# Attention scores by two products on diagonal quarters of the array instead of one with block-diagonal queries

## The chip, the cores and the metric

One core of a Trainium2 chip runs the kernel. The metric is device time in microseconds of one execution. The runs shown of the kernel before have a median of 904.97 us (904.07 to 905.69, three runs).

## What is computed

The reference is a sparse attention, followed by a layer norm with a two-matrix feed-forward part, and a routed mixture of eight experts. Inputs are fp32: q, k and v of shape (4, 8, 576, 64), that is 4 images, 8 heads, 576 positions, 64 per head. The part that the change touches is the attention:

```python
scores = scale * np.matmul(q, k.transpose(0, 1, 3, 2))
mask_local = (rel >= 0) & (rel < stride)                     # heads 0 to 3, stride 32
mask_strided = (rel >= 0) & (pos[None, :] % stride == pos[:, None] % stride)   # heads 4 to 7
scores = np.where(masks[None, :, :, :], scores, -1000000000.0)
scores = scores - np.max(scores, axis=-1, keepdims=True)
attn = np.exp(scores)
attn = attn / (np.sum(attn, axis=-1, keepdims=True) + 1e-09)
return np.matmul(attn, v).astype(np.float32)
```

## The kernel before

The attention works on pairs of heads: image `b` and pair `hp`, where pairs 0 and 1 are local heads and pairs 2 and 3 strided ones. `GROUPS` (line 36) cuts a pair into units. A local pair has 3 units of three products, each product of 64 queries by 96 keys. A strided pair, whose positions are sorted by their remainder, has units of four, four and three products, each of 54 queries by 54 keys. An image has thus 12 units, and the four images 48.

For each pair `prep` (line 270) transposes q and k on TensorE, in two halves of 288 positions, through the PSUM tile `ps_tr`. k goes to `kT`, with both heads' 64 dimensions one above the other on 128 partitions. q goes to `qbd`, scaled: a tile with two columns per position, where head 0 fills the upper 64 partitions of the even columns and head 1 the lower 64 partitions of the odd columns. The rest of `qbd` is zero, set once at the start (lines 182 to 187). Each half of q is evacuated by two instructions, one per head (lines 290 to 294): ScalarE and then VectorE or ScalarE.

`st_scores` (line 311) makes one product of the full array for both heads (line 324): the weights are 128 columns of `qbd` for local pairs and 108 for strided ones, and `kT` moves. For images 0 and 1 a mask product goes ahead of them and the scores add to it (line 320, `MODES` in line 39); for images 2 and 3 VectorE adds the mask (line 342). The rows of a score tile alternate between the heads. `st_exp`, `st_norm` (lines 346 and 356) make the softmax. `st_trans` (line 369) transposes the weights of the softmax, 128 or 108 rows at a time, and ScalarE copies them to `pt`. `st_out` (line 385) multiplies with v: two products per group, one per head, each on 64 columns of the array, the second on PSUM partitions 64 to 127 (line 392). It reads every second column of `pt`.

Image 0 is attended first, in an order written out by hand (lines 966 to 994, kept in program order; all its instructions carry line 84). Between its steps `keep_clock` (line 300) issues filler products on an idle tile. The feed-forward part then runs over 9 chunks of 256 tokens with 16 steps each; a step has 12 products of `mm1` (line 636) and 12 of `mm2` (line 652). The units of images 1, 2 and 3 are placed between its steps by `plan` and `SPANS` (lines 51 and 1004 to 1008), and from there a scheduler orders the instructions of each engine. During the first chunks ScalarE, VectorE and GpSimd also turn the feed-forward weights from their stored form into fp32 pairs (lines 451 to 481). The routed experts follow from about 620 us.

Of the kernel before, what the change touches and what calls it, by code (L numbers as in the profile page):

```python
# [9 lines left out]
F32 = mybir.dt.float32  # L10
# [5 lines left out]
AF = mybir.ActivationFunctionType  # L16
ALU = mybir.AluOpType
# [5 lines left out]
B, H, S, DH = 4, 8, 576, 64  # L23
# [3 lines left out]
STR = 32  # L27
NA = S // STR
# [3 lines left out]
NTT = CT // TT  # L32
WL = 128 + NE + 1
QT = 96
SP = S + 18
GROUPS = (((0, 3), (3, 3), (6, 3)),) * 2 + (((0, 4), (4, 4), (8, 3)),) * 2
QW, KW = (64, 64, 54, 54), (96, 96, 54, 54)
SMW, PTW = 288, 432
# [4 lines left out]
SCALE = 1.0 / DH ** 0.5  # L43
NEG = -1.0e9
# [26 lines left out]
def attention_moe_moe(ctx: ExitStack, tc: tile.TileContext, q, k, v, g_ln, w_ch1, w_ch2, w_gate, w_local, w1, w2, out):  # L71
# [14 lines left out]
    pe, act, dve = Pin(nc.tensor), Pin(nc.scalar), Pin(nc.vector)  # L86
    pool, sp = nc.gpsimd, nc.sync
# [17 lines left out]
    pool.memset(mean_w, 1.0 / DM)  # L105
    mask_loc = cst.tile([128, 128], F32, name="mask_loc")
    pool.memset(mask_loc, 0.0)
    pool.affine_select(out=mask_loc, in_=mask_loc, pattern=[[-2, 128]], compare_op=ALU.is_ge, fill=-NEG, base=2 * STR, channel_multiplier=1)
    pool.affine_select(out=mask_loc, in_=mask_loc, pattern=[[2, 128]], compare_op=ALU.is_ge, fill=-NEG, base=-1, channel_multiplier=-1)
    mask_str = cst.tile([128, 3, NA], F32, name="mask_str")  # L110
    pool.memset(mask_str, 0.0)
    pool.affine_select(out=mask_str, in_=mask_str, pattern=[[-2 * NA, 3], [-2, NA]], compare_op=ALU.is_ge, fill=-NEG, base=0, channel_multiplier=1)
    pool.affine_select(out=mask_str, in_=mask_str, pattern=[[2 * NA, 3], [0, NA]], compare_op=ALU.is_ge, fill=-NEG, base=2 * NA - 1, channel_multiplier=-1)
    mask_str = mask_str.rearrange("p a b -> p (a b)")

    def high(ap):
# [57 lines left out]
        return ps_s["r"].tile(shape, F32, tag="s", name=name)  # L174


    qbds, kTs = [at_p.tile([128, SP, 2], F32, name="qbd")], [at_p.tile([128, SP], F32, name="kT")]
    spare = new_blk([128, 2048], F32, "spare")
    idle = spare[:, 1792:2048].bitcast(BF16)
    qbds.append(spare[:, 0:2 * SP].rearrange("p (s j) -> p s j", j=2))  # L180
    kTs.append(spare[:, 2 * SP:3 * SP])
    for qbd, kT in zip(qbds, kTs):
        pool.memset(qbd[0:64, :, 1], 0.0)
        pool.memset(qbd[64:128, :, 0], 0.0)
        pool.memset(qbd[0:64, S:SP, 0], 0.0)
        pool.memset(qbd[64:128, S:SP, 1], 0.0)
        pool.memset(kT[:, S:SP], 0.0)
    nat, vt, qTs = {}, {}, {}
    xts = {}

# [79 lines left out]
    def prep(b, hp, nm):  # L270

        odd = b == 0 and pairs.index((b, hp)) % 2
        qbd, kT = qbds[odd], kTs[odd]
        qTs[b, hp] = qbd, kT
        for half in range(2):
            t = nat.pop((nm, b, hp, half))
            ps = (ps_m.tile([128, 512], F32, tag="m", name="ps_tr")[:, 0:3 * QT] if b == 0 else side_r([128, 3 * QT], "ps_tr"))
            for i in range(3):
                pe.transpose(ps[:, QT * i:QT * i + QT], t[0:QT, i, :, :].rearrange("p h d -> p (h d)"), ident[0:QT, 0:QT])

            def dst(ap):
                if hp < 2:
                    return ap[:, 3 * QT * half:3 * QT * half + 3 * QT]
                return ap.rearrange("p (r a) -> p r a", a=NA)[:, :, NA // 2 * half:NA // 2 * half + NA // 2]

            s_ = ps if hp < 2 else ps.rearrange("p (a r) -> p r a", r=STR)
            if nm == "k":
                (act.copy if b == 0 else dve.tensor_copy)(dst(kT[:, 0:S]), s_)
            else:
                act.activation(dst(qbd[0:64, 0:S, 0]), s_[0:64], AF.Copy, scale=-SCALE)  # L290
                if half and b:
                    act.activation(dst(qbd[64:128, 0:S, 1]), s_[64:128], AF.Copy, scale=-SCALE)
                else:
                    dve.tensor_scalar(dst(qbd[64:128, 0:S, 1]), s_[64:128], -SCALE, None, op0=ALU.mult)

    sms, pts = {}, {}
    first, units = [], [0, 0]
# [5 lines left out]


    def shape_of(hp, u0):
        return dict(GROUPS[hp])[u0], QW[hp], KW[hp], 2 * QW[hp]

    def mode_of(b, hp):
        return MODES.get((b, hp), MODES.get(b, 0))
# [1 line left out]
    def st_scores(b, hp, u0):  # L311
        ng, w, n, m = shape_of(hp, u0)
        ps = side([128, ng, n], "ps_sc")
        qbd, kT = qTs[b, hp]
        mode = mode_of(b, hp)
        mask = lambda i: mask_str[0:m, 0:n] if hp > 1 else mask_loc[:, STR:STR + n] if u0 + i == 0 else mask_loc[:, 0:n]
        if mode:
            cuts = [(0, 1), (1, ng)] if hp < 2 and u0 == 0 else [(0, ng)]
            for lo, hi_ in cuts:
                pe.matmul(ps[0:m, lo:hi_, :], high(ident[0:m, 0:m]), high(mask(lo)).unsqueeze(1).to_broadcast([m, hi_ - lo, n]), start=(lo == 0), stop=False)  # L320
        for i in range(ng):
            q0 = w * (u0 + i)
            k0 = max(0, q0 - STR) if hp < 2 else q0
            pe.matmul(ps[0:m, i, :], qbd[:, q0:q0 + w, :].rearrange("p s j -> p (s j)"), kT[:, k0:k0 + n], start=not mode, stop=not mode or i == ng - 1)  # L324
        if b == 0:
            k = units[0] % SM0 * SMW
            sm = first[0][:, k:k + ng * n]
            units[0] += 1
        else:
            sm = at_p.tile([128, SMW], F32, tag="sm", bufs=SMB, name="sm")[:, 0:ng * n]  # L330
        sm = sm.rearrange("p (g n) -> p g n", g=ng)
        st = at_p.tile([128, 2, 4], F32, tag="st", bufs=5, name="st")
        sms[b, hp, u0] = (sm, st, ps)
        mn = st[0:m, 0, 0:ng]
        if mode:
            new = [lambda: dve.tensor_reduce(mn, ps[0:m], axis=AX.X, op=ALU.min)]
            if mode == 1:
                new.append(lambda: dve.tensor_tensor(sm[0:m], ps[0:m], mn.unsqueeze(2).to_broadcast([m, ng, n]), op=ALU.subtract))
            return new

        def part(i):
            dve.tensor_tensor_reduce(sm[0:m, i, :], ps[0:m, i, :], mask(i), 1.0, 3.0e38, ALU.add, ALU.min, st[0:m, 0, i:i + 1])  # L342

        return [lambda i=i: part(i) for i in range(ng)]
# [24 lines left out]
    def st_trans(b, hp, u0):  # L369
        sm, st, ps = sms.pop((b, hp, u0))  # L370
        ng, w, n, m = shape_of(hp, u0)
        ps = side([128, ng, m], "ps_pt")
        for i in range(ng):
            pe.transpose(ps[0:n, i, :], sm[0:m, i, :], ident[0:m, 0:m])
        if b == 0:
            k = SM0 * SMW + units[1] % PT0 * PTW
            pt = first[0][:, k:k + ng * m]
            units[1] += 1
        else:
            pt = at_p.tile([128, PTW], F32, tag="pt", bufs=2, name="pt")[:, 0:ng * m]  # L380
        pt = pt.rearrange("p (g m) -> p g m", g=ng)
        act.copy(pt[0:n], ps[0:n])
        pts[b, hp, u0] = pt

    def st_out(b, hp, u0):
        ng, w, n, m = shape_of(hp, u0)
        pt, vv = pts.pop((b, hp, u0)), vt.pop((b, hp, u0))
        ps = side([128, ng, w], "ps_o")
        for i in range(ng):
            k = min(w, S - w * (u0 + i)) if hp > 1 else w  # L390
            for j in range(2):
                pe.matmul(ps[64 * j:64 * j + 64, i, 0:k], vv[0:min(n, k) if hp > 1 else n, i, j, :], pt[0:min(n, k) if hp > 1 else n, i, j:2 * k:2], start=True, stop=True)
        o = ps.rearrange("p g q -> p (g q)")
        i = 0
        q0 = w * u0
        nq = min(w * ng, S - q0)
        for c in range(S * b // CT, (S * b + S - 1) // CT + 1):
            base = S * b - CT * c
            if hp < 2:
                lo, hi_ = max(q0, -base), min(q0 + nq, CT - base)  # L400
                if lo >= hi_:
                    continue
                dst = xt_of(c)[:, hp, base + lo:base + hi_]
                cut = lambda t: t[:, lo - q0:hi_ - q0]
            else:
                lo, hi_ = max(0, -base // STR), min(NA, (CT - base) // STR)
                r0, nr = q0 // NA, nq // NA
                dst = xt_of(c)[:, hp, base + STR * lo:base + STR * hi_].rearrange("p (a r) -> p r a", r=STR)[:, r0:r0 + nr, :]
                cut = lambda t: t[:, 0:nq].rearrange("p (r a) -> p r a", a=NA)[:, :, lo:hi_]
            (dve.tensor_copy if (i % 2 if b else mode_of(b, hp) > 1) else act.copy)(dst, cut(o))  # L410
            i += 1
        if b > 0:
            load_v(vq.index((b, hp, [g[0] for g in GROUPS[hp]].index(u0))) + 3)
# [1074 lines left out]
```

## Time and profile before

| | |
|---|---|
| median of the runs shown | 904.97 us |
| profiled execution | 902.98 us |
| its span, from the first instruction to the last | 901.2 us |
| mean granted TensorE clock | 0.983 |
| TensorE busy, products | 867.3 us (96%) |
| TensorE busy, weight loads | 777.3 us (86%) |
| VectorE busy | 474.5 us (53%) |
| ScalarE busy | 365.6 us (41%) |
| GpSimd busy | 152.2 us (17%) |

PE is TensorE's products, PEld its weight loads, DVE is VectorE, ACT is ScalarE, POOL is GpSimd, SP issues DMAs. A product record's duration includes the pipe behind it, so neighbours overlap; what a record costs is the distance to the next start. An fp32 product has two records, a transpose one. The granted clock is 1.00 at 2.4 GHz and 0.50 at 1.2 GHz.

### The profile page before, as it was taken

To read this page: it belongs to the slowest core of one execution; us is meant where nothing else is said; L and a number is where in the kernel's file an instruction comes from. 1 tells how busy PE (TensorE), PEld (TensorE's weight loads), DVE (VectorE), ACT (ScalarE), POOL (GpSimd) and SP (SyncE) were. 2 spreads that over 40 slices of the span, in tenths; PEclk is the share of its full clock that TensorE was granted. 3 is DMA by queue.
4 is the path that set the end of the run, shared out by engine and by line. 5 is a ranking of instruction groups with operands and counts; after the bars stand their busy time and mean duration, and the time that the engine had idled before them with its cause. 6 is when DMAs were issued, how large, how long until landed. Compare 5 with 4: busy or idle time off the path is not lost. (4 is left out here: it accounts for less than half of the span.)

```text
span 901.2 us, 17965 instructions
## 1 busy us (share of the span) xinstructions
PE 867.3 (96%) x6668; PEld 777.3 (86%) x6668; DVE 474.5 (53%) x1520; ACT 365.6 (41%) x879; POOL 152.2 (17%) x163
## 2 busy tenths in 40 slices
PE   8989888999999999999999999999999999999995
PEld 5769788999999999999999999999878787787763
DVE  4877775448766546666545555667521233111541
ACT  3688878433455234354211212332122334223550
POOL 2124323211120120120201212020231211110100
PEclk9999999899999999999999999999999999999997
DMA  9836244101212102211000000510663466410730
GB/s 190 250 106 207 59 141 121 50 14 52 65 39 46 48 10 64 47 26 39 1 1 25 1 25 6 207 49 24 239 225 101 150 218 215 139 37 24 291 113 15
DMA packets 95023, 82.91 MB, mean 92 GB/s; under 512 B 67395, under 2 KB 75589, under 8 KB 94920
## 3 DMA queue, kind: packets, MB, share of 16 engines
q1 hardware_dynamic: 87656, 65.41, 24.5%
q0 software_dynamic: 3632, 11.11, 3.7%
q10 hardware_dynamic: 3632, 5.09, 1.6%
q8 instruction: 55, 0.90, 0.4%
q14 instruction: 48, 0.39, 0.1%
HBM read 72.08 MB, written 10.30 MB: 91 GB/s over the span
## 5 line engine op out<-in xcount | busy, mean ns | idle before, releaser
L652 PE MATMUL acc<-h,w 128*128 128x256 f32 x1728 | 247.5, 291 | 1.6 <-DVE h L639 1.5
L636 PE MATMUL ps_h<-xc,w 128*128 128x256 f32 x1728 | 239.6, 287 | 0.0
L652 PEld LDWEIGHTS acc<-h,w 128*128 128x128 f32 x1728 | 220.7, 192 | 5.1 <-DVE h L639 2.5
L636 PEld LDWEIGHTS ps_h<-xc,w 128*128 128x128 f32 x1728 | 221.6, 194 | 1.7
L638 ACT ACTIVATE h<-ps_h 128x256 fp32r<-128x256 f32 x144 | 55.6, 387 | 218.3 <-PE ps_h L636 203.7
L639 DVE SCALAR_TENSOR_TENSOR h<-ps_h,h 128x256 fp32r<-128x256 f32 x144 | 60.6, 421 | 94.2 <-ACT h L638 93.5
L1367 PE MATMUL ps_h<-wx,xs 128*128 128x512 f32 x360 | 87.6, 398 | 0.8 <-DVEq L1294 0.8
L1395 PE MATMUL ps_y<-wx,ht 128*128 128x512 f32 x360 | 87.5, 399 | 0.0
L1367 PEld LDWEIGHTS ps_h<-wx,xs 128*128 128x128 f32 x360 | 66.6, 188 | 15.8 <-DVEq L1294 1.2
L1395 PEld LDWEIGHTS ps_y<-wx,ht 128*128 128x128 f32 x360 | 67.6, 191 | 13.8
L481 POOL TENSOR_TENSOR w<-stg,w 128x512 fp32r<-128x512 f32 x32 | 45.6, 1424 | 120.7 <-ACT w L480 74.5
L1398 ACT ACTIVATE y<-ps_y,pr 128x512 f32<-128x512 f32 x19 | 13.1, 687 | 90.5 <-PE ps_y L1395 54.9
L890 DVE TENSOR_TENSOR xs<-ps_tx,xs 128x512 fp32r<-128x512 f32 x15 | 10.4, 691 | 63.0 <-ACTq L1294 44.8
L1370 ACT ACTIVATE h<-ps_h 128x512 f32<-128x512 f32 x30 | 16.3, 595 | 60.8 <-PE ps_h L1367 60.8
L782 DVE TENSOR_TENSOR wx<-raw,wx 128x1024 fp32r<-128x1024 f32 x32 | 37.5, 1220 | 1.7 <-ACT wx L779 1.3
L460 ACT ACTIVATE stg<-stg 128x512 f16<-128x512 f32 x27 | 37.2, 1377 | 0.6 <-DVE stg L454 0.6
L1399 POOL DMA_INDIRECT out_dram<-y,idx x15 | 15.1, 1007 | 114.6 <-ACT y L1398 66.1
L779 ACT CAST wx<-raw 128x1024 fp32r<-128x1024 f32 x32 | 31.8, 1061 | 5.7 <-PE acc L652 4.1
L354 ACT ACTIVATE sm<-sm,st 108x54 f32<-108x54 f32 (+1 forms) x80 | 27.6, 347 | 13.5 <-DVE st L342 13.4
L1384 DVE TENSOR_TENSOR ht<-ps_th,ht 128x512 fp32r<-128x512 f32 x30 | 19.3, 685 | 24.5 <-ACT ht L1383 24.1
L324 PE MATMUL ps_sc<-kT,qbd 128*108 128x54 f32 (+1 forms) x240 | 30.5, 267 | 0.0
L892 DVE SCALAR_TENSOR_TENSOR pr<-io_e,e_rep,xg 128x8 f32<-128x8 f32 x15 | 3.4, 226 | 51.2 <-ACT y L1398 46.0
(393 smaller groups left out, 1233.7 us busy)
## 6 DMA issues: line engine op xcount, KB each, us to landing
stg<-in_moe_w_ch_dram SPq DMA_DIRECT2D x32, 512.0 KB
raw<-in_moe_w_dram SPq DMA_DIRECT2D x16, 1024.0 KB
raws<-in_moe_w_dram SPq DMA_DIRECT2D x16, 1024.0 KB
xrows<-row ACTq DMA_DIRECT2D x9, 520.0 KB
qnat<-in_q_dram SPq DMA_DIRECT2D x48, 72.0 KB
knat<-in_k_dram SPq DMA_DIRECT2D x48, 72.0 KB
v<-in_v_dram SPq DMA_DIRECT2D x24, 72.0 KB
v<-in_v_dram SPq DMA_DIRECT2D x72, 18.0 KB
```

Source lines behind the costliest of these rows:

```text
L324: pe.matmul(ps[0:m, i, :], qbd[:, q0:q0 + w, :].rearrange("p s j -> p (s j)"), kT[:, k0:k0 + n], start=not mode, stop=not mode or i == ng - 1)
L354: act.activation(sm[0:m, i, :], (ps if mode else sm)[0:m, i, :], AF.Exp, bias=st[0:m, 0, i:i + 1], scale=-1.0, **({} if mode else dict(acc ...
L460: keep(act.activation(t.bitcast(F16)[..., 1], f32(t[..., 1]), AF.Copy, scale=2.0 ** -112))
L481: keep(pool.tensor_tensor(w[:, 1], r, f32(w[:, 0]), op=ALU.subtract))
L636: pe.matmul(ps, w[:, a, d, o:o + 128], xcs[c][:, b_, d, :], start=(i == 0), stop=(i == 11))
L638: act.activation(h[:, 0, :], ps, AF.Relu)
L639: dve.scalar_tensor_tensor(h[:, 1, :], ps, 0.0, f32(h[:, 0, :]), op0=ALU.max, op1=ALU.subtract)
L652: pe.matmul(accs[c][d // 2][:, d % 2, :], w[:, a, f % 2, d * 128:(d + 1) * 128], h[:, b_, :], start=(f == 0 and (a, b_) == (0, 0) and d % ...
L779: act.copy(wx[i][:, 0, :], raw[i // 2][:, i % 2, :])
L782: dve.tensor_tensor(wx[i][:, 1, :], raw[i // 2][:, i % 2, :], f32(wx[i][:, 0, :]), op=ALU.subtract)
L1367: pe.matmul(hp_[fg], s_[:, a, d, :], wx[d][:, b_, 512 * fg:512 * fg + 512], start=(i == 0), stop=(i == 11))
L1395: pe.matmul(ps, s_[a][:, f, :], wx[4 + f // 2][:, b_, 512 * (f % 2):512 * (f % 2) + 512], start=(i == 0), stop=(i == 23))
```

## The change

q is kept like k: a tile `qT` with both heads one above the other, without the zeros, of 608 columns where `qbd` had 594 times two. One instruction evacuates each half, VectorE in image 0 and ScalarE in the others. A score product becomes two, one per head: 64 weights from partitions 0 to 63 (or 64 to 127), results on PSUM partitions 0 to 63 (or 64 to 127). For strided pairs 64 queries are loaded although 54 count, so their tiles have 128 rows instead of 108; the surplus rows are masked wholly and left out when `pt` is copied. The rows of a tile are now ordered by head and not alternating, so the masks are built per half (eight selects on 64 partitions instead of four on 128), and `st_out` reads `pt` without stride. Four long memsets of zeros fall away.

```diff
-SP = S + 18
+SP = S + 32
...
-    pool.affine_select(out=mask_loc, in_=mask_loc, pattern=[[-2, 128]], compare_op=ALU.is_ge, fill=-NEG, base=2 * STR, channel_multiplier=1)
...
+    for j in range(2):
+        m = mask_loc[64 * j:64 * j + 64, :]
+        pool.affine_select(out=m, in_=m, pattern=[[-1, 128]], compare_op=ALU.is_ge, fill=-NEG, base=STR, channel_multiplier=1)
...
-    for qbd, kT in zip(qbds, kTs):
-        pool.memset(qbd[0:64, :, 1], 0.0)
-        pool.memset(qbd[64:128, :, 0], 0.0)
-        pool.memset(qbd[0:64, S:SP, 0], 0.0)
-        pool.memset(qbd[64:128, S:SP, 1], 0.0)
-        pool.memset(kT[:, S:SP], 0.0)
+    for ab in qks:
+        for t in ab:
+            pool.memset(t[:, S:SP], 0.0)
...
-        qbd, kT = qbds[odd], kTs[odd]
-        qTs[b, hp] = qbd, kT
+        qT, kT = qTs[b, hp] = qks[odd]
...
+            elif b == 0:
+                dve.tensor_scalar(dst(qT[:, 0:S]), s_, -SCALE, None, op0=ALU.mult)
             else:
-                act.activation(dst(qbd[0:64, 0:S, 0]), s_[0:64], AF.Copy, scale=-SCALE)
-                if half and b:
-                    act.activation(dst(qbd[64:128, 0:S, 1]), s_[64:128], AF.Copy, scale=-SCALE)
-                else:
-                    dve.tensor_scalar(dst(qbd[64:128, 0:S, 1]), s_[64:128], -SCALE, None, op0=ALU.mult)
+                act.activation(dst(qT[:, 0:S]), s_, AF.Copy, scale=-SCALE)
...
-        return dict(GROUPS[hp])[u0], QW[hp], KW[hp], 2 * QW[hp]
+        return dict(GROUPS[hp])[u0], QW[hp], KW[hp], 128
...
-            pe.matmul(ps[0:m, i, :], qbd[:, q0:q0 + w, :].rearrange("p s j -> p (s j)"), kT[:, k0:k0 + n], start=not mode, stop=not mode or i == ng - 1)
+            for j in range(2):
+                h = slice(64 * j, 64 * j + 64)
+                pe.matmul(ps[h, i, :], qT[h, q0:q0 + 64], kT[h, k0:k0 + n], start=not mode, stop=not mode or i == ng - 1)
...
-        pt = pt.rearrange("p (g m) -> p g m", g=ng)
-        act.copy(pt[0:n], ps[0:n])
+        pt = pt.rearrange("p (g j q) -> p g j q", g=ng, j=2)
+        act.copy(pt[0:n], ps[0:n].rearrange("p g (j q) -> p g j q", j=2)[:, :, :, 0:w])
...
-                pe.matmul(ps[64 * j:64 * j + 64, i, 0:k], vv[0:min(n, k) if hp > 1 else n, i, j, :], pt[0:min(n, k) if hp > 1 else n, i, j:2 * k:2], start=True, stop=True)
+                pe.matmul(ps[64 * j:64 * j + 64, i, 0:k], vv[0:min(n, k) if hp > 1 else n, i, j, :], pt[0:min(n, k) if hp > 1 else n, i, j, 0:k], start=True, stop=True)
```

## Rows read from the trace of the kernel before

**Rows 1.** Busy by stage: stretch, length, each engine (instructions), clock, DMA share, GB/s.

```profile
30.00:44.00 14.00, 13.89 (x148) 10.17 (x146) 12.93 (x41) 10.67 (x23) 2.82 (x2) 1.00 0.84 213
...
120.00:200.00 80.00, 74.67 (x645) 70.48 (x646) 41.74 (x104) 47.37 (x93) 19.52 (x15) 0.91 0.27 70
200.00:300.00 100.00, 100.00 (x961) 97.62 (x959) 70.54 (x313) 47.28 (x174) 11.96 (x11) 1.00 0.19 48
300.00:430.00 130.00, 128.68 (x1206) 125.91 (x1206) 77.29 (x316) 50.89 (x186) 14.75 (x15) 1.00 0.15 39
```

**Rows 2.** Timeline of TensorE, image 2, local scores: start, length, line, tiles, records.

```profile
242.57 0.81 PE L324 MATMUL ps_sc<-kT,qbd 128*128 128x96 f32 x6
243.16 1.68 PE L652 MATMUL acc<-h,w 128*128 128x256 f32 x12
244.68 1.60 PE L636 MATMUL ps_h<-xc,w 128*128 128x256 f32 x12
246.12 0.49 PE L374 MATMUL ps_pt<-iw,sm 128*96 128x128 f32 x3
246.44 0.81 PE L324 MATMUL ps_sc<-kT,qbd 128*128 128x96 f32 x6
```

**Rows 3.** The same timeline around output products, image 3 and image 0.

```profile
352.58 1.68 PE L652 MATMUL acc<-h,w 128*128 128x256 f32 x12
354.19 0.92 PE L392 MATMUL ps_o<-pt,v 96*64 96x64 f32 x24
355.05 1.70 PE L636 MATMUL ps_h<-xc,w 128*128 128x256 f32 x12
356.58 0.58 PE L279 MATMUL ps_tr<-iw,qnat 96*128 96x96 f32 x5
...
55.07 0.57 PE L84 MATMUL ps_o<-first,v 96*64 96x64 f32 x12
...
55.57 1.25 PE L84 MATMUL idle_ps<-spare 128*128 128x512 bf16 x5
```

**Rows 4.** The same timeline, transposes of 96 columns in image 0.

```profile
11.23 0.66 PE L84 MATMUL ps_tr<-iw,qk 96*128 96x96 f32 x6
11.73 0.60 PE L84 MATMUL idle_ps<-spare 128*128 128x512 bf16 x2
```

**Rows 5.** The same timeline, a strided unit of image 3.

```profile
411.60 0.44 PE L374 MATMUL ps_pt<-iw,sm 108*54 108x108 f32 x3
411.88 0.88 PE L324 MATMUL ps_sc<-kT,qbd 128*108 128x54 f32 x8
412.59 0.70 PE L672 MATMUL ps_x<-iw,xt 128*128 128x137 f32 x4
```

**Rows 6.** Stretch 57 to 200 us: evacuation (ns min/median/max), TensorE's waits (us, times, longest).

```profile
L294 DVE TENSOR_SCALAR qbd<-ps_tr x4: 462/464/466, 69.1 to 152.7; 64x288 f32<-64x288 f32 x4
...
PE ps_tr L279 <- ACT qbd L292: 0.9, 2, 0.7
...
PE ps_tr L279 <- DVE qbd L294: 0.8, 2, 0.6
```

**Rows 7.** Timeline of image 0's start; in brackets idle time and what ended it.

```profile
13.63 0.83 DVE L84 TENSOR_SCALAR spare<-ps_tr 64x288 f32<-64x288 f32 x2 [1.20 <-ACT spare L84]
...
17.93 0.93 PE L84 MATMUL ps_sc<-spare 128*108 128x54 f32 x8 [1.55 <-ACT spare L84]
```

**Rows 8.** Timeline, GpSimd's last start work and the first mask product.

```profile
7.35 0.12 POOL L187 MEMSET spare<- 128x18 f32 x1
...
8.37 0.29 PE L84 MATMUL ps_sc<-mask_loc,iw 128*128 128x96 bf16 x2
```

**Rows 9.** Image 1: the stretch at half clock (columns as above) and TensorE's gaps.

```profile
153.30:163.60 10.30, 10.30 (x68) 9.32 (x69) 4.03 (x10) 6.07 (x12) 1.30 (x1) 0.50 0.31 70
...
151.48 0.47 PE L279 MATMUL ps_tr<-iw,qnat 96*128 96x96 f32 x3 [1.17 <-ACT pt L382]
...
153.26 0.72 PE L279 MATMUL ps_tr<-iw,knat 96*128 96x96 f32 x3 [0.57 <-DVE qbd L294]
```

More of the change, by code (lines that the diff above doesn't have):

```diff
@@ L107, in attention_moe_moe @@
     pool.memset(mask_loc, 0.0)
-    pool.affine_select(out=mask_loc, in_=mask_loc, pattern=[[-2, 128]], compare_op=ALU.is_ge, fill=-NEG, base=2 * STR, channel_multiplier=1)
-    pool.affine_select(out=mask_loc, in_=mask_loc, pattern=[[2, 128]], compare_op=ALU.is_ge, fill=-NEG, base=-1, channel_multiplier=-1)
     mask_str = cst.tile([128, 3, NA], F32, name="mask_str")
     pool.memset(mask_str, 0.0)
-    pool.affine_select(out=mask_str, in_=mask_str, pattern=[[-2 * NA, 3], [-2, NA]], compare_op=ALU.is_ge, fill=-NEG, base=0, channel_multiplier=1)
-    pool.affine_select(out=mask_str, in_=mask_str, pattern=[[2 * NA, 3], [0, NA]], compare_op=ALU.is_ge, fill=-NEG, base=2 * NA - 1, channel_multiplier=-1)
+    for j in range(2):
+        m = mask_loc[64 * j:64 * j + 64, :]
+        pool.affine_select(out=m, in_=m, pattern=[[-1, 128]], compare_op=ALU.is_ge, fill=-NEG, base=STR, channel_multiplier=1)
+        pool.affine_select(out=m, in_=m, pattern=[[1, 128]], compare_op=ALU.is_ge, fill=-NEG, base=-1, channel_multiplier=-1)
+        m = mask_str[64 * j:64 * j + 64]
+        pool.affine_select(out=m, in_=m, pattern=[[-NA, 3], [-1, NA]], compare_op=ALU.is_ge, fill=-NEG, base=0, channel_multiplier=1)
+        pool.affine_select(out=m, in_=m, pattern=[[NA, 3], [0, NA]], compare_op=ALU.is_ge, fill=-NEG, base=NA - 1, channel_multiplier=-1)
     mask_str = mask_str.rearrange("p a b -> p (a b)")
@@ L174, in side_r @@
         return ps_s["r"].tile(shape, F32, tag="s", name=name)
-    qbds, kTs = [at_p.tile([128, SP, 2], F32, name="qbd")], [at_p.tile([128, SP], F32, name="kT")]
+    qks = [(at_p.tile([128, SP], F32, name="qT"), at_p.tile([128, SP], F32, name="kT"))]
     spare = new_blk([128, 2048], F32, "spare")
     idle = spare[:, 1792:2048].bitcast(BF16)
-    qbds.append(spare[:, 0:2 * SP].rearrange("p (s j) -> p s j", j=2))
-    kTs.append(spare[:, 2 * SP:3 * SP])
-    for qbd, kT in zip(qbds, kTs):
-        pool.memset(qbd[0:64, :, 1], 0.0)
-        pool.memset(qbd[64:128, :, 0], 0.0)
-        pool.memset(qbd[0:64, S:SP, 0], 0.0)
-        pool.memset(qbd[64:128, S:SP, 1], 0.0)
-        pool.memset(kT[:, S:SP], 0.0)
+    qks.append((spare[:, 0:SP], spare[:, SP:2 * SP]))
+    for ab in qks:
+        for t in ab:
+            pool.memset(t[:, S:SP], 0.0)
     nat, vt, qTs = {}, {}, {}
@@ L313, in st_scores @@
         ps = side([128, ng, n], "ps_sc")
-        qbd, kT = qTs[b, hp]
+        qT, kT = qTs[b, hp]
         mode = mode_of(b, hp)
@@ L376, in st_trans @@
             k = SM0 * SMW + units[1] % PT0 * PTW
-            pt = first[0][:, k:k + ng * m]
+            pt = first[0][:, k:k + 2 * ng * w]
             units[1] += 1
         else:
-            pt = at_p.tile([128, PTW], F32, tag="pt", bufs=2, name="pt")[:, 0:ng * m]
-        pt = pt.rearrange("p (g m) -> p g m", g=ng)
-        act.copy(pt[0:n], ps[0:n])
+            pt = at_p.tile([128, PTW], F32, tag="pt", bufs=2, name="pt")[:, 0:2 * ng * w]
+        pt = pt.rearrange("p (g j q) -> p g j q", g=ng, j=2)
+        act.copy(pt[0:n], ps[0:n].rearrange("p g (j q) -> p g j q", j=2)[:, :, :, 0:w])
         pts[b, hp, u0] = pt
```

## The prediction

> **What bounds the kernel now.** I read the busy time by stage first, since the chain that ended last holds only the final stores and says nothing of the attention. Image 0 of the attention runs up to about 56 us, image 1 up to 200, images 2 and 3 up to 430, spread between the products of the first feed-forward part. In the stretches of images 2 and 3 TensorE is never idle: 100.00 us of 100 and 128.68 of 130, at full clock [rows 1]. There every nanosecond of TensorE work that the change adds or takes away shows in the time, and nothing on ScalarE or VectorE does. The stretch 30 to 44 us of image 0 is nearly as full (13.89 of 14), but filler products stand among its work, and VectorE has 12.93 of 14. The stretch 120 to 200 us is different: TensorE idles 5.3 us there, and its granted clock is 0.91 on the mean [rows 1]. Image 1's stage is thus paced partly by ScalarE and VectorE.
>
> **The score products themselves.** Every fp32 product is two records in the trace. A local group (three products of 128 weights by 96 keys) is 6 records. From its start at 242.57 to the transposes at 246.12 are 3.55 us; 24 records of the feed-forward stand in that stretch, and 12 of them take 1.44 us when nothing intervenes (244.68 to 246.12). The score group is thus worth 3.55 - 2.88 = 0.67 us, 111 ns a record [rows 2]. It is the weight load that sets this: transposes that move the same 96 columns come every 83 ns (0.50 us for 6) [rows 4]. A strided group of four products of 108 weights by 54 keys takes 0.71 us from start to start [rows 5]; by the local group's excess over its bare start-to-start I take 0.75, and three quarters of it, 0.56, for a group of three.
>
> The change makes 12 records of each 6: two heads, 64 weights each, on the quarters at rows and columns 0 to 63 and 64 to 127. The trace of before has no such quarters on the diagonal. The nearest rows are the output products, which already put two heads on 64 columns each. There 12 records take 0.50 us and 24 records 0.86, so 12 more cost 0.36: the two heads run side by side, one pair of records every 60 ns or a little less (I use 58) [rows 3]. For the local scores the pair lasts as long as its 96 moving columns, 83 ns [rows 4], so 6 pairs need 0.50 us; 8 strided pairs need 0.46, and 6 need 0.35. Taken by themselves these would save 0.17, 0.29 and 0.21 us a group.
>
> **What leaving the full array costs.** The same output rows show the other side. From 352.58 to 356.58 stand 12 feed-forward records, 24 output records and 12 feed-forward records. The first 12 take 1.61 us where the like 12 behind a score group take 1.52 (243.16 to 244.68); output and second dozen take 2.39, of which 1.44 is the dozen. The output group is worth 0.09 + 0.95 = 1.04 us, and its 12 pairs explain only 12 x 0.058 = 0.70 [rows 2, 3]. The remaining 0.34 us is paid on entering and leaving the split array: the pipe empties, and the first weights on both sides load with nothing to hide behind. The Trainium skill, TensorEngine Tiling (Array Packing), section Key Properties, says that changing the tiling mode drains TensorE, against the gain that the same page promises for small operands; this trace agrees, with 0.34 us for one excursion.
>
> Today the score products stand in the full array between other full-array work. After the change each group becomes an excursion of its own, because transposes, feed-forward products and masks stand around it. Per group: local 0.50 + 0.34 - 0.67 = +0.17; strided of four 0.46 + 0.34 - 0.75 = +0.05; of three 0.35 + 0.34 - 0.56 = +0.13. An image has 6, 4 and 2 of them: 1.02 + 0.20 + 0.26 = +1.5 us. What is not measured here is the excursion's price at this place. If the pull-ahead of weights works better between separate rows it could fall to nothing, and the scores of an image would gain 6 x 0.17 + 4 x 0.29 + 2 x 0.21 = 2.6; the upper end is a serial pair, priced below. I keep 0.34, since the output products are the same kind of switch on the same neighbours.
>
> **The transposes.** The strided groups keep their scores on 128 rows instead of 108, so each of an image's 22 transposes moves 128 columns of the identity. Three of 108 take 0.28 us, 93 ns each [rows 5]; three of 128 take 0.32, 107 each [rows 2]. That is +14 to +18 ns, 0.3 us an image. The copy behind them still moves 2 x 54 columns a product, the reductions and exponentials work on more partitions with the same free size; I cost these at nothing. The mask products of images 0 and 1 get 20 more weight columns, under 20 ns each.
>
> **Sum for images 2 and 3:** 2 x (1.5 + 0.3) = +3.6 us, all on the path [rows 1].
>
> **The evacuation of q.** It becomes one instruction for both heads. Image 1's four pairs each lose one ScalarE instruction and one VectorE instruction of 464 ns [rows 6]; the latter waited for the former, since both read the same buffer. TensorE stood 0.9 + 0.8 us on these two before it could transpose k [rows 6]. I count these 1.7 us as gained (at least 0, if the weight conversion that fills ScalarE is late next; at most 1.7 plus 4 x 0.46 of pace). Of image 1's own +1.8 on TensorE half falls into idle gaps. Image 1: +0.9 - 1.7 = -0.8.
>
> In image 0, VectorE evacuates q alone and no longer waits for ScalarE: at 13.63 it stood 1.20 us for that, and the chain behind it (normalisation, next minimum, exponential, k copy) holds TensorE for 1.55 us at 17.93 [rows 7]. I take 1.2 of it back. The extra TensorE time of image 0 counts while TensorE is full there, up to about 44 us: I take +1.0 of the 1.8. What is late next are the weight conversions after 44 us, which neither of these moves. Image 0: -0.2 (between -1 and +1). GpSimd's four additional mask selects replace four long memsets; its start work ends at 7.35, before the first mask product at 8.37 [rows 8], with less to do afterwards. Nothing here, and no queue of DMAs is moved.
>
> **Sum:** 3.6 - 0.8 - 0.2 = +2.6 us. Against the profiled execution (902.98, a span of 901.2 plus 1.8 around it) this is 905.6. That execution lay 2.0 below the median of the runs shown, 904.97; on that median the forecast is 907.6.
>
> **The rivals.** *The clock.* TensorE was granted half speed (1.2 of 2.4 GHz) for 10.3 us from 153.3 on; just there k's transposes had waited 0.57 us for VectorE's half of q, after other gaps [rows 9]. The change takes that wait away. If the stretch then stays at full clock, up to half of it comes back, 5 us: 907.6 - 5 = 902.6, faster than before. It decides from whether this one wait is what tips the clock; a longer one at 151.5 waits for another copy and stays. Chance 0.27.
>
> *The quarters don't run side by side.* Both heads write the same PSUM bank from different rows. Each record would then take its own step: 6 x 0.50 + 4 x 0.46 + 2 x 0.35 = 5.5 us more an image, some 20 over the four with part of images 0 and 1 hidden: 927. Against it speaks that output pairs in one bank already overlap [rows 3], though they share their rows. The Trainium skill, TensorEngine Tiling (Array Packing), Gotcha 1, says that different row tiles cannot access one PSUM bank at the same time; by that rule it is this rival, and no run here shows such tiles yet. Chance 0.10.
>
> *Broken groups.* The scheduler places other products between the two heads of some groups, or a new gap brings another short stretch at half clock. Each break costs another 0.34, each 3.4 us at half clock 1.7: 910 to 912. Chance 0.08.
>
> *Image 1 swallows it.* Its +1.8 hides wholly and ScalarE's pace improves as well: 904.97 + 3.6 - 0.2 - 3.5 = 904.9, no change. Chance 0.08. The forecast keeps 0.47.
>
> **How the numbers follow.** A measurement can tell about 0.2%, 1.8 us, from no change: below 903.2 is faster, above 906.8 slower. The forecast's own range is 905 to 911 (images 2 and 3 between 3.0 and 4.4, the two others between -2 and +2 together); 0.10 of its 0.47 is within 0.2%. The clock rival gives 0.24 faster and 0.03 same, the swallowing rival 0.07 same and 0.01 faster, the others are slower. Faster 0.25, same 0.20, slower 0.55. Leaving out the serial rival and the far tail of the clock's, the range is 901 to 912.5.
>
> **What would show it.** In the profile after: score records in 64-column form, pairs starting together every 58 or 83 ns; a local group between two feed-forward dozens worth 0.84 us instead of 0.67; the dozen before it 0.09 longer. Images 2 and 3 should end later than image 1 ends by 3.6 us more than now. The waits of k's transposes on q should be gone. If groups are worth 1.3 us, the quarters are serial; if they are worth 0.5, the excursion is free, and I am wrong by some 8 us. If the clock stretch from 153 is gone, the sign may turn.

## The result and the profile after

The changed kernel takes 896.42 us (median of 6 runs, 894.21 to 899.25) against 904.52 for the kernel before beside it (6 runs): a ratio of 0.9902, interval 0.9876 to 0.9927. I had forecast 907.6 and a range of 901.0 to 912.5. The profiled execution took 897.15 us with a span of 895.4, 5.8 less than before's 901.2.

The page of the profile after, part 1: busy time, share of the span, instructions.

```profile
span 895.4 us, 18585 instructions
...
PE 864.9 (97%) x6988; PEld 764.8 (85%) x6988; DVE 467.0 (52%) x1508; ACT 356.2 (40%) x859; POOL 149.5 (17%) x161
```

Where the 5.8 us lie is read from the start of the same feed-forward step in both traces. The first step marks the end of image 0, step 24 the end of image 1, steps 36 and 88 enclose images 2 and 3.

| stretch | before | after | difference | forecast |
|---|---|---|---|---|
| image 0, to the first step | 56.91 | 53.84 | -3.1 | -0.2 |
| image 1, to step 24 | 120.23 | 117.28 | -3.0 | -0.8 |
| steps 24 to 36 | 40.62 | 40.29 | -0.3 | 0 |
| images 2 and 3, steps 36 to 88 | 213.75 | 214.67 | +0.9 | +3.6 |
| the rest of the span | 469.7 | 469.3 | -0.4 | 0 |

So the signs of all three parts were as forecast, and all three came out 2.2 to 2.9 us below the forecast. The windows by stage (columns as in [rows 1]) show that images 2 and 3 are as full as before:

```profile
30.00:44.00 14.00, 13.97 (x160) 8.61 (x159) 13.43 (x38) 11.76 (x23) 3.80 (x3) 1.00 0.85 212
120.00:200.00 80.00, 75.04 (x743) 70.19 (x744) 46.69 (x114) 49.24 (x102) 22.11 (x19) 1.00 0.27 70
200.00:300.00 100.00, 100.00 (x1040) 94.77 (x1039) 67.48 (x309) 43.06 (x164) 10.10 (x9) 1.00 0.22 56
300.00:430.00 130.00, 129.13 (x1278) 123.72 (x1277) 75.07 (x315) 48.52 (x179) 16.12 (x16) 1.00 0.13 33
```

The row that differs is 120 to 200: the granted clock is 1.00 where [rows 1] had 0.91. The half-clock stretch of [rows 9] is gone; what is left of such stretches in image 1 is one of 10.3 us at 93.4:

```profile
93.40:103.70 10.30, 9.70 (x45) 9.39 (x46) 5.90 (x22) 5.46 (x10) 2.60 (x2) 0.50 0.01 2
148.00:164.00 16.00, 14.44 (x168) 13.14 (x167) 10.02 (x28) 12.20 (x25) 4.49 (x4) 1.00 0.37 95
```

In all, image 1 has 10.2 us at half clock after and 20.5 before (from 64.6, 95.3, 122.6 and 153.3). TensorE's idle time hardly changed there: its busy time, taken from the length of image 1, leaves 9.9 us before and 9.7 after. What fell is its busy time, by 2.8 us, though it has more records (before, then after):

```profile
56.91:177.14 120.23, 110.34 (x919) 104.09 (x917) 84.71 (x203) 93.81 (x163) 39.99 (x29) 0.91 0.37 108
53.84:171.11 117.27, 107.59 (x1000) 98.67 (x999) 81.55 (x199) 90.76 (x159) 38.99 (x29) 0.96 0.40 111
```

At the start of image 0 the stall of [rows 7] is gone. The timeline there (start, length, engine, line, tiles; idle time in brackets):

```profile
11.39 0.81 DVE L84 TENSOR_SCALAR spare<-ps_tr 128x288 f32<-128x288 f32 x2
...
15.58 0.67 PE L84 MATMUL ps_sc<-spare 64*64 64x54 f32 x16
```

VectorE no longer waits before it evacuates q (1.20 us before), and the strided pair's scores start 15.58, with no idle time ahead, instead of 17.93 after 1.55.

TensorE's waits in the stretch 57 to 200 us (total, times, longest), the stretch of [rows 6], and the evacuation of q that now stands in one line:

```profile
PE ps_pt L372 <- DVE sm L361: 2.2, 1, 2.2
PE ps_o L390 <- ACT pt L380: 1.8, 3, 0.9
PE acc L650 <- DVE h L637: 1.5, 3, 1.0
PE ps_tr L277 <- ACT pt L380: 1.3, 1, 1.3
```

```profile
L290 ACT ACTIVATE qT<-ps_tr x24: 387/420/527, 61.2 to 396.0; 128x288 f32<-128x288 f32 x24
```

The two waits on `qbd` of [rows 6] are gone. Other waits grew, for `h` from 0.8 to 1.5 us in all. One instruction on 128 partitions takes 420 ns at the median, no more than one on 64 took before (441 on ScalarE; [rows 6] has 464 for VectorE's half).

### The profile page after: what moved, and what is told of

Read it like the earlier page. It is cut to its first block, busy times and chain, and to the rows that moved or that the text cites. A ratio compares the mean times of both kernels' runs of the same rounds, so it can differ in the third digit from the quotient of the medians.

```text
span 895.4 us, 18585 instructions
## 1 busy us (share of the span) xinstructions
PE 864.9 (97%) x6988; PEld 764.8 (85%) x6988; DVE 467.0 (52%) x1508; ACT 356.2 (40%) x859; POOL 149.5 (17%) x161
## 5 line engine op out<-in xcount | busy, mean ns | idle before, releaser
L634 PE MATMUL ps_h<-xc,w 128*128 128x256 f32 x1728 | 236.7, 286 | 0.1
L634 PEld LDWEIGHTS ps_h<-xc,w 128*128 128x128 f32 x1728 | 219.3, 193 | 2.1 <-DVE xc L618 0.5
L352 ACT ACTIVATE sm<-sm,st 128x54 f32<-128x54 f32 (+1 forms) x80 | 27.6, 347 | 13.5 <-DVE st L340 13.5
L867 POOL DMA_INDIRECT xg<-xrows,idx x16 | 16.3, 1020 | 56.0 <-PE ps_y L1393 33.7
```

Source lines behind the costliest of these rows:

```text
L352: act.activation(sm[0:m, i, :], (ps if mode else sm)[0:m, i, :], AF.Exp, bias=st[0:m, 0, i:i + 1], scale=-1.0, **({} if mode else dict(acc ...
L634: pe.matmul(ps, w[:, a, d, o:o + 128], xcs[c][:, b_, d, :], start=(i == 0), stop=(i == 11))
```

## The experiments

Two theories. **E**: the gain comes from the evacuation of q by one instruction, and the quarters are about neutral. **Q**: the quarters are the gain. A third, **C**, was that the granted clock differs by chance. The runs of the kernel before beside the variants, in three batches, have means of 903.20 to 903.27 us, so that variants of different batches can be compared.

### One part alone, first attempt

```diff
                 act.activation(dst(qbd[0:64, 0:S, 0]), s_[0:64], AF.Copy, scale=-SCALE)
-                if half and b:
-                    act.activation(dst(qbd[64:128, 0:S, 1]), ...)
-                else:
-                    dve.tensor_scalar(dst(qbd[64:128, 0:S, 1]), ...)
```

> The kernel before, with its full-array score product on block-diagonal queries, but only the first head's half of q is evacuated, by the one ScalarE instruction; the second head's queries stay zero (one memset more on GpSimd at the start), so the scores of the second head are left out of the computation. TensorE's work is that of the kernel before, instruction for instruction. Theory E (the gain of the change comes from q's evacuation: one instruction instead of two, the first pair's chain in image 0, the stalls and the half-clock stretches in image 1): most of the 8 us is there without any quarters, 893 to 898 us, image 0 ending 2 to 3 us earlier and at least one of the half-clock stretches of image 1 gone. Rival Q (the quarters themselves are the gain): 902 to 906, as before. Rival C (the granted clock of image 1 varies by itself, whatever is changed): somewhere between, with the time following the granted clock and not the edit.

Measured: 960.37 us (5 runs), which says nothing on the question. With half the queries at zero the tokens are routed otherwise, and the expert part is longer; its products on the page number 384 where before had 360:

```profile
L1364 PE MATMUL ps_h<-wx,xs 128*128 128x512 f32 x384 | 95.1, 403 | 3.4 <-ACTq L1291 3.2
```

I should have seen that the data of the scores decide how much work comes later. Up to there the trace can be read: image 0 ends at 54.17 (before 56.91), image 1 at 168.60 (before 177.14). Without any quarters, 8.5 us are gained by then. That is for E, but the time of the whole had to be shown with all data in place.

### One part alone, all data in place

```diff
-                act.activation(dst(qbd[0:64, 0:S, 0]), ...)      # and the second head's instruction
+                    dve.tensor_tensor(o_, s_.unsqueeze(2).to_broadcast(sh), hm.unsqueeze(1).to_broadcast(sh), op=ALU.mult)
```

> The kernel before with its full-array product on block-diagonal queries, all data in place, but q evacuated by one VectorE instruction: the transposed queries times a two-column constant (-scale for the head's own rows, 0 for the others) into both interleaved columns, twice the elements; the long memsets of zeros go. TensorE's work is that of the kernel before. Unlike the run that left the second head out, the routing and so the expert products are the same. Theory E (one instruction in the chain is the gain): image 0 ends 1.5 to 3 us earlier, image 1's waits of the transposes of k go or halve, 895 to 900 us. If the gain came from the quarters: 902 to 905. VectorE's instruction is longer (an estimate of 0.65 us, from 0.46 for half its elements, as fixed cost is part of it), so up to 2 us of the 7 may be lost.

Measured: 896.19 us (7 runs), ratio to before 0.9929, interval 0.9898 to 0.9961. As far as the intervals tell, the old full-array product with one evacuation instruction is as fast as the change. That instruction takes 743 to 761 ns here, against 420 in the change, and the first strided scores wait 0.70 us in place of 1.55; the line and the timeline:

```profile
L294 DVE TENSOR_TENSOR qbd<-ps_tr,hm x12: 743/747/757, 68.3 to 353.4; 128x576 f32<-128x576 f32 x12
```

```profile
16.88 0.96 PE L84 MATMUL ps_sc<-spare 128*108 128x54 f32 x8 [0.70 <-ACT spare L84]
```

In image 0 the expectation missed: it ends at 56.19, 0.7 us earlier than before and not 1.5 to 3. It holds 3.4 us at half clock from 46.9 on, a stretch that image 0 has neither in the kernel before nor in the changed one:

```profile
46.94:50.35 3.41, 3.41 (x20) 1.82 (x21) 3.27 (x8) 2.57 (x4) 1.42 (x1) 0.50 0.98 337
```

Image 1 takes 116.32 us, 3.9 less than before. Another 2.2 of the 6.8 us by which this profile is shorter lie behind step 88, where the code is the same, with 4.4 us at half clock instead of 10.6. So the two kernels with one instruction are equally fast, but did not gain in the same places.

### The other part alone

```diff
+                act.activation(dst(qT[0:64, 0:S]), s_[0:64], AF.Copy, scale=-SCALE)
+                if half and b:
+                    act.activation(dst(qT[64:128, 0:S]), s_[64:128], AF.Copy, scale=-SCALE)
+                else:
+                    dve.tensor_scalar(dst(qT[64:128, 0:S]), s_[64:128], -SCALE, None, op0=ALU.mult)
```

> The changed kernel with its quarters, but q is evacuated by two instructions for each half as in the kernel before: rows 0 to 63 by ScalarE, then rows 64 to 127 by VectorE (in the second half of images 1 to 3 by ScalarE). Theory E: 902 to 907 us, the two kernels' difference gone: image 0 ends about 3 us later than in the changed kernel, image 1's waits on q are back. Rival Q: 895 to 898, as the changed kernel. My forecast's own parts say +3.6 for the quarters in images 2 and 3 and -1 to -3 for the evacuation: 906 to 908 here. Rival C: follows the granted clock.

Measured: 903.26 us (12 runs) against 903.28 for before: ratio 1.0004, interval 0.9991 to 1.0018. With the quarters and the old evacuation nothing is gained. Image 0 ends at 56.14, 2.3 us later than in the changed kernel; its wait is back, and so is TensorE's wait on q in image 1, where TensorE is idle for 12.0 us instead of 9.7:

```profile
13.11 0.84 DVE L84 TENSOR_SCALAR spare<-ps_tr 64x288 f32<-64x288 f32 x2 [1.16 <-ACT spare L84]
...
17.32 0.67 PE L84 MATMUL ps_sc<-spare 64*64 64x54 f32 x16 [1.24 <-ACT spare L84]
```

```profile
PE ps_tr L277 <- ACT qT L290: 1.0, 2, 0.9
```

Together these make a table of two by two, in medians: 903.3 and 903.3 with two instructions, 896.2 and 895.1 to 896.4 with one, the full array first and the quarters second. E holds for the time as a whole, Q falls. The four long memsets are not the gain, since the run with quarters and two instructions leaves them out as well. Nor is the choice of the engine, since the one instruction is VectorE's throughout in the full-array kernel, and VectorE's and ScalarE's in the change.

### Image 0 alone, and images 1 to 3 alone

The edit of the last run, under `b == 0` and under `b > 0`.

> The changed kernel, with q evacuated by two instructions (ScalarE rows 0 to 63, VectorE rows 64 to 127) in image 0 alone. Theory E: image 0 ends 2.5 to 3.5 us later than in the changed kernel, and the time follows: 898 to 900 us, if the granted clock of image 1 stays as it is. My forecast priced this part at -1.2 of a stall (0.2 in the sum): 896.5 to 898. Rival C: image 0's end moves, and the phase of the half-clock stretches of image 1 moves with it, so that 5 us come or go: 896 or 903.

> The changed kernel, with q evacuated by two instructions in images 1 to 3 and by one in image 0: the complement of the run that did this for image 0 alone (897.75 us, 1.3 over the changed kernel, though its image 0 ended 3.4 us later). If the two parts add up, the remaining 5.5 of the 7 us are here: 901 to 902.5 us. If one part hides behind the other (a later end of image 0 is absorbed by image 1's waits), 903, as with both. If the first run's small price means that the evacuation matters little in either place: 897 to 898.

Measured: 897.75 (10 runs) and 899.68 (12 runs). The first is below E's 898 to 900 and inside the 896.5 to 898 of my forecast's own price. Image 0 ends at 57.22 there, 3.4 us after the changed kernel. It holds 3.4 us at half clock, from 48.0 on; in the run before this, with the same code in image 0 and no such stretch, image 0 ended 2.3 later. By the end of image 1 only 1.5 are left (172.58 against 171.11): image 1 took 115.37 us there and 117.28 in the changed kernel, with the same code. So in this pair of profiles a little under half of a difference in image 0 comes through. Images 1 to 3 hold the larger share. The two prices, 1.3 to 2.6 and 3.3 to 4.6 by which median of the changed kernel one takes, make up most of the 7; I had expected 901 to 902.5 for the second run, and its 899.68 is below.

### Heads one after the other

```diff
-        for i in range(ng):
-            for j in range(2):
+        for j in range(2):
+            for i in range(ng):
```

> The changed kernel with the head loop outside the product loop: all products of head 0 on rows and columns 0 to 63, then all of head 1 on the other diagonal quarter. Neighbours in the order then share a quarter, and nothing runs side by side but at the one border. If it is the alternation of heads that makes two quarters run at once: local groups worth about 0.5 us more each, strided about 0.3, some 4 us an image, and 10 to 14 us in all after what images 0 and 1 hide: 906 to 911 us. If the quarters overlap over a longer queue, or the weight load alone sets the pace: 896 to 899 as the changed kernel.

Measured: 899.60 us (one run), between the two ranges that I had expected; images 2 and 3 took 219.71 us against 214.67. The same group in both timelines, first this run, then the changed kernel:

```profile
240.84 0.93 PE L322 MATMUL ps_sc<-kT,qT 64*64 64x96 f32 x12
241.69 0.31 PE L725 MATMUL ps_oo<-iw,oo 40*128 40x40 f32 x2
```

```profile
240.59 0.71 PE L322 MATMUL ps_sc<-kT,qT 64*64 64x96 f32 x12
241.23 0.32 PE L725 MATMUL ps_oo<-iw,oo 40*128 40x40 f32 x2
```

From the group's start to the next product it is 0.85 us against 0.64: 0.21 more, in 11 of the 12 local groups. The strided groups of four cost 0.27 more and those of three 0.16, and the 24 groups together are the 5.0. So the quarters do overlap, and alternating the heads matters. But even in this order they overlap in part. The group's records are two chains with like steps, one for each head; the second starts 222 ns after the first, right behind the third record and not behind the sixth. That is why a local group costs 0.21 more and not the 0.5 that I had expected.

### Filling TensorE's waits

```diff
+        if (b, hp, u0) == (1, 0, 0):
+            for _ in range(24):
+                pe.matmul(ps[:, 0, :], high(ident), high(ident), start=True, stop=True)
```

and 14 more ahead of q's second half in image 1's last pair, once in the changed kernel and once in the one before.

> The changed kernel, plus 38 short bf16 products of the identity by itself that nothing reads: 24 ahead of the first transposes of image 1, where TensorE stood 2.24 us for VectorE at 89.9, and 14 ahead of the second half of q's transposes of its last pair, where it stood 1.25 at 148.1. Theory K (such a stand is what tips the granted clock, and half speed costs about half of its 10.2 us): the stretch 93.4 to 103.7 is gone, granted clock 0.995 or better, 891 to 894 us. Rival L (the half-clock stretches are set by something else, such as the lone one-column products at 95 to 100): the stretch stays or moves, 896 to 898. If the products themselves come after the wait and cost their own time: up to +2 us.

> The kernel before with the same 38 products at the same two places (stands of 2.26 us at 92.3 and 1.17 at 150.3, and half-clock stretches from 95.3 and from 153.3). Theory K: both stretches go, 13.7 of the 20.5 us at half clock in image 1, and 896 to 899 us without any change to the scores; then most of what the change brings is TensorE's clock, which any other means of filling the waits brings too. Rival L: 902 to 905, the stretches move elsewhere.

Measured: 901.00 us (12 runs, 4.6 more than the changed kernel's 896.42) and 904.53 (12 runs; ratio to before 1.0009, interval 0.9986 to 1.0031). Neither gained. The first timeline shows why this is no test of theory K:

```profile
90.14 1.61 PE L376 MATMUL ps_pt<-iw 128*128 128x128 bf16 x24
92.48 0.53 PE L378 MATMUL ps_pt<-iw,sm 128*96 128x128 f32 x3 [0.74 <-DVE sm L364]
...
96.57 1.65 PE L576 MATMUL ps_var<-mean_w,sq 128*128 128x1 f32 x7 [2.78 <-ACT pt L386]
...
151.50 1.00 PE L278 MATMUL ps_tr<-iw 128*128 128x128 bf16 x14 [1.25 <-ACT pt L386]
```

The first wait shrank from 2.24 to 0.74, but the next one, for ScalarE's copy, grew from 0.60 to 2.78; the nine feed-forward products that had stood there were placed elsewhere. The 14 others came only after their wait. The stretch at half clock moved from 93.4 to 95.1 and kept its length. In the kernel before, the two stretches moved from 95.3 to 98.8 (and from 3.4 to 6.8 us) and from 153.3 to 156.8. What tips the clock stays open.

### Scores behind the output products

```diff
-ORDER = "TBXAMONF"
+ORDER = "TAMOBXNF"
```

in the changed kernel and, as the control, in the full-array kernel with one evacuation.

> The changed kernel with the kinds of work inside a step in another order: scores come behind the output products, which are on split columns already, instead of between feed-forward products and transposes (ORDER TAMOBXNF for TBXAMONF). My forecast priced leaving the full array at 0.34 us an excursion, and the trace of the changed kernel shows about 0.16 beside feed-forward products and nearly nothing beside routing products on 40 rows. If that price is real, a group behind output products shares it: images 2 and 3 get 1 to 2 us shorter than in the changed kernel (from step 36 to step 88: 214.66 us there), against a change of half a us or less in the run with the same order and the full-array product. If an excursion costs nothing, both runs move alike. The time as a whole also holds image 1, whose waits the order moves too: 893 to 899.

> The same order of work (TAMOBXNF) with the full-array product on block-diagonal queries and q evacuated by one VectorE instruction: the control. Images 2 and 3 (step 36 to step 88) took 213.77 us in that kernel with the old order. With a real price of the excursion nothing to half a us is gained here, since the outputs' own excursion stays: 213.5 to 214. If the order moves both alike, 212 to 213. Time as a whole 893 to 899.

Measured: 898.98 and 900.37 us (12 runs each). Images 2 and 3 got longer in both, 216.02 and 214.89, by 1.35 and 1.12: both moved alike, and my expectation missed. The order put only four groups behind output products and most of the others behind feed-forward products. Those that did get there can be compared one by one. One local group, the quarters first, then the full array:

```profile
248.57 0.92 PE L390 MATMUL ps_o<-pt,v 96*64 96x64 f32 x24
249.41 0.71 PE L322 MATMUL ps_sc<-kT,qT 64*64 64x96 f32 x12
250.06 1.70 PE L634 MATMUL ps_h<-xc,w 128*128 128x256 f32 x12
```

```profile
249.32 0.92 PE L396 MATMUL ps_o<-pt,v 96*64 96x64 f32 x24
250.18 0.91 PE L328 MATMUL ps_sc<-kT,qbd 128*128 128x96 f32 x6
250.87 1.68 PE L640 MATMUL ps_h<-xc,w 128*128 128x256 f32 x12
```

From the output products' start to the feed-forward's start it is 1.49 us with quarters and 1.54 with the full array; between feed-forward products, below, the quarters are 0.17 dearer. The three strided groups there are 0.18 to 0.25 us shorter with quarters. So the excursion is shared where split work is next to split work. The order as a whole brings nothing.

### The changed kernel once more

> The changed kernel as it is, timed on the same chip as these two, for the comparison with the full-array kernel that evacuates q by one instruction (896.19 us). By the runs so far, of time against granted clock, the quarters cost about 2 us of work, which a higher granted clock gives back: 896 to 897 us at a granted clock of 0.990 to 0.991 on the mean, against 0.987 there. If the clock is a matter of chance alone, the mean clock of these runs is as likely 0.986 to 0.988, and the time 898 to 899.

Measured: 895.11 us (5 runs), ratio 0.9917, interval 0.9890 to 0.9944. The profile repeats the first: image 0 ends at 53.79, images 2 and 3 take 214.68 us, and image 1's one stretch at half clock stands at 93.0 to 103.3.

### Time and granted clock

Every run has its mean granted clock beside its time. A straight line with one slope and a level for each kernel, over 174 runs of ten kernels (all but the first attempt and the single run; ± is two standard errors), gives 5.6 us for 0.01 of mean granted clock. The mean clock was 0.9839 before, 0.9913 after, 0.9869 with the quarters alone and 0.9873 with the evacuation alone. At equal clock:

| step | time at equal clock | by the clock | together |
|---|---|---|---|
| quarters (on two evacuations) | +1.6 ± 0.7 | -1.7 | -0.1 |
| quarters (on one) | +1.9 ± 1.1 | -2.2 | -0.4 |
| one evacuation (full array) | -5.0 ± 0.9 | -1.9 | -6.9 |
| one evacuation (quarters) | -4.7 ± 1.0 | -2.4 | -7.1 |

Theory C falls in its plain form: the clock differs from kernel to kernel and not only from run to run. But the line doesn't say what causes what, since a run with more waiting may lose clock for that reason, and the clock's share was never switched by itself. The one slope is rough too: fitted to each kernel alone, it lies between 0.6 and 10.5 us. It is an accounting, not a cause shown.

## Why the prediction was wrong

**The score products and the excursion: right between feed-forward products, too high in the sum.** The full-array kernel with one evacuation has TensorE's work of before, and its images 2 and 3 take 213.77 us (before 213.75); it is the reference here. For each of the 24 groups I took the distance from the last record ahead of it to the second one behind it. Seven of 12 local groups cost 0.16 to 0.18 us more with quarters (forecast +0.17). The timeline of one, to set beside [rows 2]:

```profile
236.55 0.71 PE L322 MATMUL ps_sc<-kT,qT 64*64 64x96 f32 x12
237.19 1.70 PE L650 MATMUL acc<-h,w 128*128 128x256 f32 x12
```

The group's start to the feed-forward's is 0.64, against 0.59 in [rows 2]; the rest of the +0.17 is paid on the records on either side (209 ns before the first where 119 stood, 222 behind the next where 204 stood). Groups of three strided products cost 0.11 more (forecast 0.13), groups of four 0.02 to 0.04 where nothing broke them (forecast 0.05). Local groups ahead of the routing's products on 40 rows cost nothing more (-0.001 and +0.001), since the full-array group paid for that change too (206 ns to the next start, against 58 ahead of feed-forward products), and two ahead of the `ps_li` products cost 0.10. The sum is +1.8 us where I had +3.0. Counted from a group's first start to its last, 2.5 us are saved (forecast 5.2); entering costs 2.3, leaving 1.2 and the record behind 0.9, in all 0.18 a group where I had 0.34. Both terms were about twice too large by this count. I had taken 0.34 from one stretch around output products [rows 3] and put it on every group. The 83 ns that I took for a record on a quarter held: with the heads one after the other, records of one chain come 82 to 83 ns apart. That the weight load sets the full array's 111 is not shown by the transposes beside it, which load 128 columns too [rows 4].

**The transposes** of 128 columns cost +0.54 (forecast 0.6).

**"Every nanosecond shows" was not quite so.** [rows 1] has 128.68 of 130 us, and I read that as full. The missing 1.3 us are waits in image 3, for the routing and for a load of k, and 0.4 of the added work went into them. Before, then after:

```profile
366.44 0.29 PE L727 MATMUL ps_oo<-iw,oo 40*128 40x40 f32 x2 [1.07 <-DVE oo L720]
...
382.14 0.44 PE L279 MATMUL ps_tr<-iw,knat 96*128 96x96 f32 x3 [0.25 <-DMA knat<-in_k_dram]
```

```profile
361.21 0.28 PE L725 MATMUL ps_oo<-iw,oo 40*128 40x40 f32 x2 [0.87 <-DVE oo L718]
```

Another 0.9 us was saved by luck: the scheduler left two groups of 28 output records whole that stand as 18 and 10 before, which no term of mine held. All together, +0.9: five profiles of kernels with quarters, in the old order and with alternating heads, have 214.67 to 214.82 there, the one with fillers 215.65.

**Image 0** is the step that failed most: -3.1 for -0.2, in each of its terms. I took 1.2 of the 1.55 stall back; from the first mask product to the first strided scores it is 8.14 us after and 9.56 before, so 1.4 came back, because VectorE's evacuation also starts earlier. I gave back 1.0 for more TensorE work, and that doesn't show: from there to the end of image 0 it is 38.26 us after, 38.97 before, and 38.82 in the run with quarters and two instructions. Where that work went is open. It does not simply hide, since with the heads one after the other image 0, from its first mask product on, took 48.5 us instead of 46.4. And I costed the very start at nothing by looking at GpSimd [rows 8]; the first mask product stands behind the first pair's q, whose two halves were evacuated one after the other by two engines, and it starts at 7.44 instead of 8.37. About half of that 0.9 is the evacuation's: the run with quarters and two instructions has its transposes of q as early as the changed kernel and starts at 7.91. The other half is luck, and lies ahead of the evacuation. Those transposes ran at half clock before, 160 ns apart instead of 82, since the granted clock rose at 6.6 there and at 4.7 after; in six profiles with the same code up to there it rose anywhere from 4.3 to 6.8. Before, then after:

```profile
5.46 1.17 PE L84 MATMUL ps_tr<-iw,qk 96*128 96x96 f32 x6
5.34 0.69 PE L84 MATMUL ps_tr<-iw,qk 96*128 96x96 f32 x6
```

The weight conversions after 44 us, which I took to be late next, held nothing back: the strided scores moved by 2.35 us and the end of image 0 by 3.1. The run with two instructions in image 0 alone puts 3.4 us on its end, in a profile with a stretch at half clock there, and the run with quarters and two instructions throughout puts 2.3.

**Image 1**: -3.0 for -0.8. The 1.7 us of waits on q went as forecast, but as a gain the term was wrong: other waits grew (that for `h`, for one), and the idle time fell by 0.2 us only. With quarters and two instructions it is 12.0 us, in both runs that have them in image 1, so that against those one instruction saves 2.3. The difference from the kernel before is in TensorE's busy time, with half of image 1's time at half clock gone (20.5 to 10.2 us), which the forecast's sum left to a rival. By the line above these 10.2 us are worth 3.2, an estimate: half of them, over 900 us, is 0.0057 of mean clock. That the evacuation itself keeps the clock up is not shown. I halved the rest and left out the pace of ScalarE and VectorE that I had given as the upper end; no run shows these two by themselves.

**The rivals.** The clock rival had the sign: the stretch at 153.3 is gone in both profiles of the changed kernel. It went in the run with quarters and two evacuations as well, where others are longer (94.1 to 107.7), so that this wait on q tips the clock is not shown. The rival went with 902.6, and the measured time is 6 below that, because I had let it alter only the forecast's own sum, which was too high in each part. The serial rival falls: two heads write one PSUM tile from different rows and start together, 6 ns apart in the group at 236.55. The Trainium skill, TensorEngine Tiling (Array Packing), Gotcha 1, says that different row tiles cannot access one PSUM bank at the same time. These starts do not show that rule for two tiles on the diagonal. The Trainium skill, TensorEngine Tiling (Array Packing), Key Properties, says that a change of tiling mode drains TensorE. This trace agrees, with 209 ns instead of 119 on entry, and 151 where the neighbour is split (the local group behind output products above). No score group of images 2 and 3 was broken. That image 1 swallowed its own share is not shown, as its idle time did not shrink.

## What to carry to other kernels

An edit often has a part that it isn't named for. Here two instructions per half became one, on a chain that runs transposes, evacuation, scores, minimum, exponential; all of the 7 us is there, and the named part brings nothing that these runs can tell from noise. Price such a chain link by link in every stage where it paces the work, not only where one engine is seen to stand still. A wait that goes is a gain only if the idle time as a whole gets shorter, so read that too. And make the two-by-two of the parts before explaining a sum.

## What the runs showed of the hardware

- Two fp32 products on diagonal quarters run at once, with results in one PSUM tile: 6 ns between their starts, 12 records of 96 columns in 0.47 us from the first start to the last. They do so in part even when each head's products come in a row (0.69 us).
- ScalarE evacuates 128 partitions in the time that it takes for 64: 420 ns at the median, for 288 values, against 411 in the run with quarters and two instructions and 441 before.
- The same code of image 1 took 117.28 us in one profile and 115.37 in another. With 0.01 less mean granted clock a run took 5.6 us more, and one kernel had from 0.979 to 0.989 in its 12 runs.
